# Batch 0's q loaded and prepared by halves of the heads, w2 held behind batch 1's v, and three moves of loads and stores on SP's and GpSimd's queues

## The chip, the cores and the metric

The kernel runs on one core of a Trainium2 chip. The metric is the device time of one execution in microseconds (us); the time before is the median of three runs. Everything said of where time goes comes from one profiled execution. In the listings PE is the matrix engine, PEld its weight loads, DVE the vector engine, ACT the scalar engine, POOL is GpSimd, and SP is the engine that only issues DMA transfers. A "q" behind an engine's name (SPq) is its queue of issued transfers.

## The reference

Eight batches go through a linear attention with cosine weights and then through a mixer with a low-rank part and two dense layers:

```python
# attention, q, k, v of shape (8 batches, 8 heads, 576 rows, 64)
phi(x) = concat([relu(x) * cos_w, relu(x) * sin_w])      # 128 features per head
kv = k_p^T v ;  z = sum over rows of k_p
x = (q_p kv) / (q_p z + 1e-6)                            # 576 x 512 per batch
# mixer
u = x + (low-rank mix over the 576 rows: U, V, rank 32)
out = u + relu(u @ w_ch1) @ w_ch2                        # 512 -> 2048 -> 512
```

The two dense layers are most of the work of PE.

## The kernel before, in words

**Tiling.** The 576 rows of a batch are cut into five chunks: c = 0 to 3 with 128 rows and c = 4, the tail, with 64. Two batches make a pair, whose two tails share one tile. Each of q, k and v has one staging tile in SBUF (qst, kst, vst; 128 x 8 heads x 5 chunks x 64, f32) that all batches use in turn. For batches 0 and 1 it is filled by two loads (`load_odd`, `load_even`, L67 to L77), from batch 2 on by three: `load_tail` for the tail and the two of `load_main` for the other chunks (L79 to L89). All of these are issued by SP. The weights come through POOL's queue (`w1_load`, `w2_load`, L94 to L104), four loads each, with a cast to bf16 in flight.

**The front.** Batch 0 has a path of its own (L813 to L842). 22 dummy matmuls (`keep_warm`) run while q is loaded. `q_prep` then makes the features of a chunk for all eight heads: the cosine half on DVE, the sine half on ACT (on DVE for c = 3). PE transposes each chunk's eight heads (`qtr_mm`), with a dummy matmul behind each chunk; DVE and ACT move the five transposed chunks out of PSUM (`qtr_evac`). `k_prep` follows with the sums z, and `first_chain` does kv, the normalisation, the low-rank part and opens the transposed u (uT) of batch 0.

**What orders the rest.** From there on PE walks a list of slots, written out by hand (L948 to L961), and each engine executes its instructions in the order in which the program gives them. Slots 0 to 15 are the first dense layer of batch 0 (`g1_main`, one slot per 128 of the 2048 columns), 16 to 31 the second layer of batch 0 (`g2_part`, chunks 0 to 3, in four parts that each need one of w2's four loads), 32 to 47 the first layer of batch 1, 48 to 51 that of the two tails, 52 to 71 the second layer for cc = 4 (the tails) and cc = 5 to 8 (batch 1's chunks), four slots each. Slot 72 begins the next pair. Beside the slots hang the steps of the attention of later batches (`put(slot, step)`): the table `PLAN` gives for batches 2 to 7 the slot of kv and the distances of preparing q and k, of the transposes, and of the loads for the batch that follows. Batch 2's kv is at slot 46, batch 3's at 64.

**Transposes by DMA.** From batch 1 on u is transposed by DMA (`utr_dma`, L455), and from batch 2 on q too (`qtr_dma`, L339), all on SP's queue: for batch 3 the q chunks 0 and 1 at slot 59, chunks 2 and 3 at slot 65. The transpose of batch 1's u is at slots 23 and 24, that of batch 2's u at 62 and 64.

**Gates.** POOL issues w1's loads when a small copy (`mark`, L839) has read the last bytes of the first half of batch 0's v, and w2's loads when another (L850) has read the last bytes of batch 1's k. SP holds batch 2's loads at slot 15 with two small transfers that read w2 (`gate`, L867); between these it transposes batch 0's uT back to u (`u_dma`). Batch 2's q (tail and main) and k's tail follow at slot 15; the rest of k, and v, at slot 26.

**Stores.** `g2_part` adds u to the sum in PSUM on DVE (o_sb, four buffers) and stores it: pairs 0 to 2 from POOL's queue, pair 3 from SP's. POOL also casts parts of v to bf16 (`v_prep`); for batch 3 the chunks 4, 0 and 1, at slots 52, 53 and 54.

Of the kernel before, what the change touches and what calls it, by code (L numbers as in the profile page):

```python
# [17 lines left out]
def kernel(  # L18
# [11 lines left out]
    nc = tc.nc  # L30

    B = 8
    H = 8
# [9 lines left out]
    TS = 64  # L43
# [23 lines left out]
    def load_even(dst, src, b, h0=0, h1=H):  # L67
        nc.sync.dma_start(
            out=dst[0:P:2, h0:h1].rearrange("m h c d -> m h (c d)"),
            in_=nines(src, b)[:, h0:h1, 0 : 5 * D],  # L70
        )

    def load_odd(dst, src, b, h0=0, h1=H):
        nc.sync.dma_start(
            out=dst[1:P:2, h0:h1, 0:4].rearrange("m h c d -> m h (c d)"),
            in_=nines(src, b)[:, h0:h1, 5 * D : 9 * D],
        )  # L77
# [38 lines left out]
    stU = st_uv[:, S : S + 5 * R].rearrange("p (c r) -> p c r", r=R)  # L116

    zero = const.tile([P, 512], BF16)
    V_.memset(zero, 0.0)  # L119
    for x in (qst, kst, vst):  # L120
        V_.memset(x[:, :, 4, :], 0.0)
    load_odd(qst, q, 0)
    load_even(qst, q, 0)
    load_odd(kst, k, 0)
    load_even(kst, k, 0)
    for h0 in (0, 4):
# [63 lines left out]
    def keep_warm(n, tag, bufs):  # L190
        w_ps = ps.tile([P, 512], FP32, tag=tag, bufs=bufs, name="w_ps")
        for _ in range(n):
            nc.tensor.matmul(out=w_ps, lhsT=zero[:, 0:P], rhs=zero, start=True, stop=True)  # L193
# [367 lines left out]
        )  # L561

    o_ps = {}

    def g2_part(pr, cc, part):

        last = pr == NPAIR - 1 and cc == 8
        if part == 0 or last and part == 3:
            tag, bufs = ("g", 3) if pr == 0 and 2 <= cc < 4 else ("o", 2)
            o_ps[pr, cc] = ps.tile([P, DM], FP32, tag=tag, bufs=bufs, name="o_ps")  # L570
        o = o_ps[pr, cc]
        if cc == 4:
            b, lhs, c, u = None, hid_tl[pr], 0, u_tl[pr]
        else:
            b, c = (2 * pr, cc) if cc < 4 else (2 * pr + 1, cc - 5)
            lhs, u = hid[b], u_bf[b][:, c, :]

        if last:
            cols = slice(0, 384) if part < 3 else slice(384, DM)
            js = (range(0, 5), range(5, 10), range(10, NJ), range(NJ))[part]  # L580
        else:
            cols, js = slice(0, DM), range(part * 4, part * 4 + 4)
        for j in js:
            nc.tensor.matmul(  # L584
                out=o[:, cols],
                lhsT=lhs[:, j, c * P : c * P + P],
                rhs=w2_bf[:, j, cols],
                start=(j == 0),
                stop=(j == NJ - 1),
            )  # L590
        if js[-1] < NJ - 1:
            return
        o_sb = pool.tile([P, DM], FP32, tag="o_sb", bufs=4, name="o_sb")
        nc.vector.tensor_tensor(  # L594
            out=o_sb[:, cols], in0=u[:, cols], in1=o[:, cols], op=ALU.add
        )
        eng = nc.gpsimd if pr < NPAIR - 1 else nc.scalar if part == 3 and last else nc.sync
        if cc == 4:
            for i in range(2):
                eng.dma_start(  # L600
                    out=out[2 * pr + i].rearrange("(m k) n -> m k n", k=9)[:, 4, :],
                    in_=o_sb[i * TS : i * TS + TS, :],
                )
        else:
            eng.dma_start(  # L605
                out=out[b].rearrange("(m k) n -> m k n", k=9)[:, c : c + 6 : 5, cols],
                in_=o_sb[:, cols],
            )


    def loads(b):
# [29 lines left out]
    def attention_plan(b):  # L641

        plan = []
        w, f_at, q_eng, k_eng, qtr, lo = PLAN[b]

        def put(at, f, *a, tag=False):
            if tag:
                a = a + spare(w + at)
            plan.append((w + at, lambda: f(b, *a)))

        for n, c in enumerate(QORD):
            if b == 3:
                q_eng, k_eng = V_ if n == 3 else A_, A_ if n < 3 else None
                put((-12, -11, -10, -7, -3)[n], q_prep, c, (q_eng, q_eng))
                put(n - 9 if n < 3 else -5, k_prep, c, (A_, k_eng))
                if n > 2:
                    put(2 * n - 12, k_prep, c, (None, V_))
                put(-4 if n > 2 else n - 12, v_prep, 0, H, (c,), (A_ if n > 2 else G_,))
                continue
            put(f_at + n, q_prep, c, (q_eng, q_eng))  # L660
            put(f_at + 6 + n, k_prep, c, (k_eng, k_eng))
            on_v = b == 2 and n > 2
            put(
                -5 if on_v else f_at + 3 + (3 * n) // 2,
                v_prep, 0, H, (c,), (V_ if on_v else G_,),
            )
        for n, (c0, c1) in enumerate(((4, 5), (0, 2), (2, 4))):
            put(1 if b == 3 and n == 2 else qtr + 2 * n, qtr_dma, c0, c1)
        put(0, kv_unit, 0, tag=True)
        put(2, kv_unit, 1, tag=True)  # L670
        for n, c in enumerate(ORD):
            if b > 3:
                put(4 + 2 * n, x_unit, c, "X", 1)
            elif n % 2:
                put(9 if (b, n) == (3, 3) else 4 + (3 * n) // 2, x_two, c, tag=True)
            else:
                put(4 + (3 * n) // 2, x_unit, c, "X", 1)
        a_at = 12 if b < 4 else 14
        put(a_at, A_unit, tag=True)
        odd = b % 2 == 1  # L680
        for c in range(4 + odd):
            put(a_at + 2 + c, u_unit, c, tag=True)
        put(a_at + 4, utr_dma, 0, 2)
        put(a_at + 6, utr_dma, 2, 4)
        if odd:
            put(a_at + 8, utr_dma, 4, 5)
        for at, t in zip(lo, loads(b + 1) if lo else ()):
            plan.append((w + at, t))
        return plan


    TL = (0, 1, 2, 3, 4)
# [119 lines left out]

    FEATS = [(V_, V_ if c == 3 else A_) for c in TL]  # L813
    qT_alloc(0)
    keep_warm(22, "X", 1)
    t_q = []
    for c in TL:
        tg = G3 if c < 3 else O2
        t_q.append(ps.tile([P, H, P], BF16, tag=tg[0], bufs=tg[1], name="t_ps"))
    for c in TL:  # L820
        q_prep(0, c, FEATS[c])
        qtr_mm(0, c, 0, H, t_q[c])
        keep_warm(1, "X", 1)
    for c, eng in zip(TL, (V_, A_, V_, A_, V_)):
        qtr_evac(0, c, eng, t_q[c])
    keep_warm(5, "X", 1)
# [20 lines left out]
    for h0 in (0, 4):  # L847
        load_odd(vst, v, 1, h0, h0 + 4)
        load_even(vst, v, 1, h0, h0 + 4)
    G_.tensor_copy(out=mark, in_=kst[0:TS, 7, 4, 0:1])  # L850
    for n in range(4):
        w2_load(n)
    g1_main(0, 0, True)
# [111 lines left out]
    def put(at, thunk):  # L965
        todo.setdefault(at, []).append(thunk)
# [3 lines left out]
        put(15, lambda c0=c0: u_dma(0, c0, c0 + 2))  # L970
    put(15, lambda: gate(w2_bf[0:1, 4, 0:1]))
    for n, t in enumerate(loads(2)):
        if n == 1:
            put(15, lambda: load_tail(kst, k, 2))
            put(26, lambda: load_main(kst, k, 2))
        else:
            put((15, 0, 26)[n], t)
    for b in range(2, B):
        for at, t in attention_plan(b):
            put(at, t)  # L980
    for i, s in enumerate(slots):
        s()
        for t in todo.get(i, []):
            t()
# [30 lines left out]
```

## Time and profile before

| what | us |
|---|---|
| median of three runs (lowest, highest) | 309.62 (308.99, 310.02) |
| the profiled execution, in all | 310.23 |
| its span, first to last instruction | 308.5 |
| PE busy in the span | 300.3 |
| DVE, ACT, POOL busy | 149.1, 139.5, 52.3 |
| HBM read, written | 36.86 MB, 9.44 MB |

The span is the time that the traces divide; the 1.7 us around it belong to no instruction. Busy time of PE is from the start of a matmul to its modelled end, and matmuls overlap, so the pace of their starts says more than the share. "Landing" is the moment at which all parts of a transfer have signalled. An idle time with an arrow, as in `[2.09 <-DMA vst<-in_v_dram]`, is how long the engine stood before this instruction and what ended the wait. The chain of work lists the pieces that led to the last instruction: start, duration, what. The 40 slices of a row are 7.7 us each.

### The profile page before, as it was taken

To read this page: it belongs to the slowest core of one execution; us is meant where nothing else is said; L and a number is where in the kernel's file an instruction comes from. 1 tells how busy PE (TensorE), PEld (TensorE's weight loads), DVE (VectorE), ACT (ScalarE), POOL (GpSimd) and SP (SyncE) were. 2 spreads that over 40 slices of the span, in tenths; PEclk is the share of its full clock that TensorE was granted. 3 is DMA by queue.
4 is the path that set the end of the run, shared out by engine and by line. 5 is a ranking of instruction groups with operands and counts; after the bars stand their busy time and mean duration, and the time that the engine had idled before them with its cause. 6 is when DMAs were issued, how large, how long until landed. Compare 5 with 4: busy or idle time off the path is not lost.

```text
span 308.5 us, 5730 instructions
## 1 busy us (share of the span) xinstructions
PE 300.3 (97%) x2304; PEld 157.3 (51%) x2329; DVE 149.1 (48%) x354; ACT 139.5 (45%) x237; POOL 52.3 (17%) x94
## 2 busy tenths in 40 slices
PE   8989999999999999999999999999999999999995
PEld 3676464448454444574455444574455444474443
DVE  4978674873866593156336691146327510002111
ACT  2935911365770556579100466679300366630000
POOL 8411200340051007004221400004221000000000
PEclk9999999999999999999999999999999999999999
DMA  7999999999999979991999579912970140001221
GB/s 212 352 261 255 244 193 231 245 328 219 283 216 185 288 142 269 248 260 70 214 208 329 174 124 231 288 39 83 179 166 34 70 85 0 0 2 68 77 95 68
DMA packets 90253, 54.26 MB, mean 176 GB/s; under 512 B 58484, under 2 KB 87444, under 8 KB 90228
## 3 DMA queue, kind: packets, MB, share of 16 engines
q1 hardware_dynamic: 83524, 42.41, 59.7%
q0 software_dynamic: 6560, 11.43, 14.8%
q8 instruction: 18, 0.29, 0.4%
q10 hardware_dynamic: 144, 0.07, 0.1%
q14 instruction: 7, 0.06, 0.1%
HBM read 36.86 MB, written 9.44 MB: 150 GB/s over the span
## 4 chain that ended last, share of the span: by engine, by line
PE 91%; DMA 5%; DVE 2%; issue 1%; ACT 0%; SPq 0%; ACTq 0%; DVEq 0%
PE o_ps L584 38%; PE g_ps L531 36%; PE gt_ps L551 5%; DMA q_pT<-q_p 3%; PE kv_ps L299 3%; PE x_ps L390 2%; DMA qst<-in_q_dram 2%; PE va_ps L435 2%; PE t_ps L328 1%; PE a_ps L415 1%; PE t_ps L316 1%; PE w_ps L193 1%; PE z_ps L832 0%; PE va_ps L438 0%; PE x_ps L894 0%
## 5 line engine op out<-in xcount | busy, mean ns | idle before, releaser
L540 ACT ACTIVATE hid<-g_ps 128x512 bf16<-128x512 f32 x128 | 76.0, 598 | 107.5 <-PE g_ps L531 107.4
L584 PE MATMUL o_ps<-w_bf,hid 128*128 128x512 bf16 (+2 forms) x509 | 117.4, 372 | 0.9
L531 PE MATMUL g_ps<-uT,w_bf 128*128 128x512 bf16 x512 | 116.8, 379 | 0.1
L531 PEld LDWEIGHTS <-w_bf 128*128 128x128 bf16 x512 | 48.6, 98 | 57.2 <-issue 1.7
L584 PEld LDWEIGHTS <-hid 128*128 128x128 bf16 x528 | 48.5, 98 | 51.9 <-issue 1.1
L594 DVE TENSOR_TENSOR o_sb<-u_bf,o_ps 128x512 f32<-128x512 bf16 (+2 forms) x33 | 22.1, 669 | 57.0 <-PE o_ps L584 55.9
L605 POOL DMA_DIRECT2D out_dram<-o_sb x24 | 15.1, 630 | 123.0 <-DVE o_sb L594 60.0
L110 POOL CAST v_ext<-vst 128x512 bf16<-128x512 f32 (+1 forms) x26 | 19.5, 773 | 43.5 <-DMA vst<-in_v_dram 43.3
L110 DVE CAST kv<-kv_ps 128x260 bf16<-128x260 f32 (+1 forms) x15 | 6.4, 429 | 37.4 <-PE kv_ps L299 37.4
L442 DVE TENSOR_TENSOR u_bf<-x_bf,va_ps 128x512 bf16<-128x512 bf16 x24 | 16.5, 686 | 10.2 <-PE va_ps L435 10.2
L363 DVE TENSOR_SCALAR rec<-x_ps 128x8 f32<-128x8 f32 (+2 forms) x39 | 6.3, 162 | 21.2 <-PE x_ps L390 19.4
L551 PE MATMUL gt_ps<-uT_tl,w_bf 128*128 128x128 bf16 x256 | 15.9, 219 | 0.0
L400 DVE TENSOR_TENSOR x_bf<-x_ps,rec 128x512 bf16<-128x512 f32 x22 | 15.2, 692 | 0.8
L551 PEld LDWEIGHTS <-w_bf 128*128 128x128 bf16 x256 | 14.7, 98 | 0.9
L584 PE MATMUL o_ps<-w_bf,hid_tl 128*128 128x512 bf16 x61 | 14.6, 379 | 0.2
L193 PE MATMUL w_ps<-zero 128*128 128x512 bf16 x36 | 11.9, 445 | 1.3 <-DVE zero L119 1.2
L299 PEld LDWEIGHTS <-k_p 128*128 128x128 bf16 x256 | 11.2, 97 | 3.2
L558 ACT ACTIVATE hid_tl<-gt_ps 128x512 bf16<-128x512 f32 x16 | 9.6, 597 | 6.6 <-PE gt_ps L551 6.6
L258 ACT ACTIVATE k_p<-kst,sinw 128x512 bf16<-128x512 f32 x17 | 12.0, 715 | 0.0
L299 PE MATMUL kv_ps<-v_ext,k_p 128*128 128x65 bf16 (+1 forms) x256 | 11.8, 193 | 0.0
L260 DVE TENSOR_SCALAR q_p<-qst,cosw 128x512 bf16<-128x512 f32 x21 | 9.8, 477 | 3.0 <-DMA qst<-in_q_dram 3.0
L390 PEld LDWEIGHTS <-q_pT 128*128 128x128 bf16 x176 | 8.5, 98 | 4.7
(137 smaller groups left out, 245.7 us busy)
## 6 DMA issues: line engine op xcount, KB each, us to landing
qst<-in_q_dram SPq DMA_DIRECT2D x14, 512.0 KB, 5.9
kst<-in_k_dram SPq DMA_DIRECT2D x14, 512.0 KB, 8.0
out_dram<-o_sb POOLq DMA_DIRECT2D x24, 256.0 KB, 4.9
vst<-in_v_dram SPq DMA_DIRECT2D x12, 512.0 KB, 8.8
w_bf<-in_moe_w_ch_dram POOLq DMA_DIRECT2D x8, 512.0 KB, 12.6
out_dram<-o_sb SPq DMA_DIRECT2D x7, 256.0 KB, 2.4
qst<-in_q_dram SPq DMA_DIRECT2D x2, 640.0 KB, 6.5
kst<-in_k_dram SPq DMA_DIRECT2D x2, 640.0 KB
```

The source lines that it names most:

```text
L110: eng.tensor_copy(out=o, in_=i)
L193: nc.tensor.matmul(out=w_ps, lhsT=zero[:, 0:P], rhs=zero, start=True, stop=True)
L299: nc.tensor.matmul(out=acc[:, i, :], lhsT=k_of(b, c, h), rhs=v_tl[:, h, 0:n] if c == 4 and b < 2 else vx[:, c, h, 0:n], start=(c == 0), st ...
L390: nc.tensor.matmul(out=acc[:, g, i * E : i * E + E], lhsT=qT_of(b, c, h), rhs=kv_sb[b][:, h, :], start=True, stop=True,)
L400: nc.vector.tensor_tensor(out=x_of(b, c, rows).rearrange("p (g i d) -> p g i d", g=2, d=D), in0=view[:, :, :, 0:D], in1=rec[rows].unsqueez ...
L442: nc.vector.tensor_tensor(out=u_bf[b][:, c, :] if c < 4 else u_tl[b // 2], in0=x_of(b, c), in1=va, op=ALU.add,)
L531: nc.tensor.matmul(out=g_ps.rearrange("p (c t) -> p c t", c=4), lhsT=w1_bf[:, d, j * P : j * P + P], rhs=uT[b][:, :, d, :], start=(d == 0) ...
L540: nc.scalar.activation(out=hid[b][:, j, :], in_=g_ps, func=AF.Relu, bias=0.0, scale=1.0)
L551: nc.tensor.matmul(out=g_ps[:, jj, :], lhsT=w1_bf[:, d, j * P : j * P + P], rhs=uT_tl[pr][:, d, :], start=(d == 0), stop=(d == 3),)
L584: nc.tensor.matmul(out=o[:, cols], lhsT=lhs[:, j, c * P : c * P + P], rhs=w2_bf[:, j, cols], start=(j == 0), stop=(j == NJ - 1),)
L594: nc.vector.tensor_tensor(out=o_sb[:, cols], in0=u[:, cols], in1=o[:, cols], op=ALU.add)
L605: eng.dma_start(out=out[b].rearrange("(m k) n -> m k n", k=9)[:, c : c + 6 : 5, cols], in_=o_sb[:, cols],)
```

## The change

The change has five parts.

1. Batch 0's q is loaded in four transfers instead of two, heads 0 to 3 first; the zeroing of the staging tile is cut in the same way, the first half ahead of everything. Features and transposes of q are made for heads 0 to 3 of all five chunks, then for heads 4 to 7. There are 10 dummy matmuls ahead instead of 22, and six between instead of five.
2. w2's loads wait for the first half of batch 1's v instead of batch 1's k.
3. Batch 2: of q only the main part is loaded at slot 15; q's tail and all of k go to slot 26 with v, behind the transposes of batch 1's u. The tail of q is prepared last instead of first.
4. Batch 3's casts of v on POOL move from slots 52 to 54 to slot 58.
5. Of pair 0, the stores of cc = 5, 6 and 7 go to SP's queue; those of 5 and 6 are kept back until slot 65, where they follow batch 3's last transpose of q.

```diff
     zero = const.tile([P, 512], BF16)
+    V_.memset(qst[:, 0:4, 4, :], 0.0)
     V_.memset(zero, 0.0)
-    for x in (qst, kst, vst):
+    V_.memset(qst[:, 4:8, 4, :], 0.0)
+    for x in (kst, vst):
         V_.memset(x[:, :, 4, :], 0.0)
-    load_odd(qst, q, 0)
-    load_even(qst, q, 0)
+    for h0 in (0, 4):
+        load_odd(qst, q, 0, h0, h0 + 4)
+        load_even(qst, q, 0, h0, h0 + 4)
...
+    late = []
...
-        else:
+            return
+
+        def store():
             eng.dma_start(
                 out=out[b].rearrange("(m k) n -> m k n", k=9)[:, c : c + 6 : 5, cols],
                 in_=o_sb[:, cols],
             )
+
+        if pr == 0 and 5 <= cc < 8:
+            eng = nc.sync
+            if cc < 7:
+                late.append(store)
+                return
+        store()
...
-                put(-4 if n > 2 else n - 12, v_prep, 0, H, (c,), (A_ if n > 2 else G_,))
+                put(-4 if n > 2 else -6, v_prep, 0, H, (c,), (A_ if n > 2 else G_,))
                 continue
-            put(f_at + n, q_prep, c, (q_eng, q_eng))
+            put(f_at + ((n - 1) % 5 if b == 2 else n), q_prep, c, (q_eng, q_eng))
...
-    keep_warm(22, "X", 1)
+    keep_warm(10, "X", 1)
...
-    for c in TL:
-        q_prep(0, c, FEATS[c])
-        qtr_mm(0, c, 0, H, t_q[c])
-        keep_warm(1, "X", 1)
+    for h0 in (0, 4):
+        for c in TL:
+            q_prep(0, c, FEATS[c], h0, h0 + 4)
+            qtr_mm(0, c, h0, h0 + 4, t_q[c])
+            if c % 2 == 0:
+                keep_warm(1, "X", 1)
...
-    G_.tensor_copy(out=mark, in_=kst[0:TS, 7, 4, 0:1])
+    G_.tensor_copy(out=mark, in_=vst[0:TS, 3, 4, 0:1])
     for n in range(4):
         w2_load(n)
...
     for n, t in enumerate(loads(2)):
-        if n == 1:
-            put(15, lambda: load_tail(kst, k, 2))
-            put(26, lambda: load_main(kst, k, 2))
-        else:
-            put((15, 0, 26)[n], t)
+        if n == 0:
+            put(15, lambda: load_main(qst, q, 2))
+            put(26, lambda: load_tail(qst, q, 2))
+        else:
+            put(26, t)
...
+    put(65, lambda: [store() for store in late])
```

## The prediction

> **What bounds the kernel.** I read the page's first two parts, then PE's waits, then the chain of work in order of time, and last the timelines of POOL and SP where the diff touches them. In the page, PE and its clock are full in every slice but the first and the last:
>
> ```profile
> PE 300.3 (97%) x2304; PEld 157.3 (51%) x2329; DVE 149.1 (48%) x354; ACT 139.5 (45%) x237; POOL 52.3 (17%) x94
> PEclk9999999999999999999999999999999999999999
> ```
>
> From 23 us on PE issues a 512-column matmul each 0.216 us (56 of L531 in 12.19 us from 58.38). A change that takes no matmul away gains only where PE stands still. PE's waits list four places, one of them deep in the kernel; the timeline's chain shows it, and the front in which PE is fed by the loads of batch 0:
>
> ```profile
> PE x_ps L894 <- DMA q_pT<-q_p: 0.7, 1, 0.7
> PE xh_ps L709 <- DVE rec L364: 0.5, 1, 0.5
> ```
>
> ```profile
> 1.70 5.67 DMA qst<-in_q_dram
> 7.48 0.73 ACT q_p L258
> ...
> 12.17 0.89 DVE k_p L260 x2
> 13.09 0.34 PE z_ps L832 x8
> ...
> 23.04 0.43 PE g_ps L531 x2
> ...
> 91.74 9.02 DMA q_pT<-q_p
> 100.81 0.43 PE x_ps L894 x8
> ```
>
> So there are two stretches to win from, the front (0 to 23 us) and the place at 98 to 101 us. All else can only lose.
>
> **1. The place at 98 to 101.** Batch 3's transpose of q chunks 2 and 3 is issued by SP at 91.74 and lands at 100.77, 9.0 us later. The same transpose of batch 4 is issued at 120.77 and lands 4.3 us later, that of batch 2 (68.16) 5.1 us. Just ahead of the slow one stands the transpose of batch 2's u (90.36), 7.8 us to landing, against 4.1 us for batch 1's (52.56). What is different is POOL's list:
>
> ```profile
> 87.71 1.17 POOL L110 CAST v_ext<-vst 128x512 bf16<-128x512 f32 x2 [2.09 <-DMA vst<-in_v_dram]
> 88.83 1.10 POOL L600 DMA_DIRECT2D out_dram<-o_sb  x2
> 89.91 1.28 POOL L605 DMA_DIRECT2D out_dram<-o_sb  x2
> 94.92 0.63 POOL L605 DMA_DIRECT2D out_dram<-o_sb  x1 [3.73 <-DVE o_sb L594]
> ```
>
> The stores of the tails, finished at 81.97, sat behind casts that waited for batch 3's v, and went out with those of cc 5 and 6 onto the transposes. The change puts the casts behind the tails' store (slot 58, that store is slot 55), and cc 5 to 7 on SP behind the transpose (slots 65, 67), in the same ring. I take 5 us for it (bounds 4.3 and 9.0): landed at 96.7. PE wants it at 99.94, eight matmuls after 98.20. PE's start there, 98.20, itself waited for batch 2's uT, landed at 98.15: the step before it ended a matmul slot at 97.96. Gain: 0.24 + (100.81 - 99.94) = **1.11 us**, if PE comes there no later. The two stores held until slot 65 keep two of four o_sb buffers; cc 7 and 8 take the others (cc 8 that of the tails, stored by then), and the next use is at slot 108, so nothing waits. SP gets three issues of 0.65 us ahead of batch 4's loads, but its 6.06 us transpose shrinks by more.
>
> **2. q in halves.** Now the first q_p starts at 7.48, when all q is there (1.70 + 5.67). Packets flow at 350 GB/s and SP's issues (0.65 us each, two more) run 4 us ahead of the data, so the second half lands at 7.4 as before and k where it did (11.15 by its completion signals). The first half lands the second's data time earlier (576 KB at 350 GB/s, 1.7 us): at about 5.7, after cosw (5.02). Per half DVE does six and ACT four instructions. At 128x512 they follow each other every 0.40 and 0.61 us; casts of half width every 0.20 and 0.31 us. So they are through at 7.5 + 6x0.20 = 8.7 instead of 9.92, and after three and two evacuations (0.60, 0.95) at 10.6; before it was 12.17 and 11.82. Then k is late, 11.15: DVE starts it at 11.3, 0.9 us earlier. The path from there to PE's 22.88 is DVE's six k_p, its v casts, and PE and DVE by turns, none of them changed; v's second half (14.46) is wanted at 14.5. So the chain offers 0.9 us (0.5 to 1.1).
>
> The dummy matmuls fall from 22 to 10: first one at 1.45 (zero's memset goes behind one of 0.27 us), 0.43 us each, last end 5.75. In the timeline they are 0.43 us apart until 5.00 and 0.22 from 5.36, so ten are just past the change of rate. If the rate came 3 us later, forty transposes at 0.11 and warm-ups at 0.43 would end near 10.6, still before k: no cost.
>
> **3. What is late next: w1.** The first w1 load (issued 13.03) lands at 13.03 + 8.9 = 21.9, and PE wants it at 22.88. Batch 1's k load, now issued at 14.51, follows batch 0's k_p: it moves to 13.5. Its packets came 3.9 us after the issue (the queue is nearly empty from 17.2 to 18.4), and from then on w1 runs at 117 packets per us instead of 190. One microsecond less alone costs w1 about 0.5: landing 22.4. So only **0.4 us** of the 0.9 reach PE at 23 (bounds 0 and 0.95, the latter if k's packets don't move).
>
> **4. w2 held.** POOL's gate goes from k of batch 1 (28.95) to the first half of v:
>
> ```profile
> 29.07 0.18 POOL L850 COPY mark<-kst 64x1 f32<-64x1 f32 x1 [12.59 <-DMA kst<-in_k_dram]
> 29.52 2.97 POOL L102 DMA_DIRECT2D w_bf<-in_moe_w_ch_dram  x4 [0.27 <-issue]
> ```
>
> That v load, issued at 16.62, lands 16.8 us later, 33.4; with k's loads a microsecond earlier, 32.4. The issue comes 0.57 us later: 33.0. w2's first load took 9.2 us from 29.52 to 38.7, but behind w1 and beside v; a free queue needs some 3.0 us to the first packet (stores: 2.3 to 3.6), 2.6 of data (w2's next loads land 2.5 apart) and up to 1.5 for the last engine: 6.4 to 7.7. So it lands at 39.4 to 40.7; bounds 38.0 and 43.2 (34.0 + 9.2). PE's first o_ps is at 40.57, now 40.2. I take no stall, or 0.4: it eats at most what w1 left. Nothing else stands behind the copy on POOL until 55.6; on SP, the gate on w2 delays u_dma and batch 2's q by about 1.2 us, with 3 us of slack (u_dma lands at 50.44, read at 54.63). Later w2 loads are needed 4 us apart. Batch 1's v gains, but DVE's 2.99 us wait for it cost PE nothing.
>
> **5. Tails behind the transposes.** Two issues of 0.65 us go from before SP's 51.20 to behind 54.63, ahead of batch 2's k and v. DMA is idle at 56.0 to 57.2 (58 GB/s) and absorbs half: v lands 0.5 us later (67.4 to 67.9). q's tail is now prepared last; its transpose waits for SP anyway (63.40). DVE's casts and k_p for kv at 70.41 end at 69.73: 70.2 now. SP is busy without a break to 87.8, so batch 3's v also comes 0.5 us later, and the tails' stores, now under its load, add 0.66. POOL's casts, which end at 88.88, end at 90.0; kv wants them at 89.93. Gain of the front that passes here: **about 0**, with bounds -0.6 and +0.4.
>
> **Sum.** 308.5 - 1.11 - 0 = 307.4 us of span. The profiled execution took 310.23 in all, 1.7 more than its span and 0.6 above the median; on the median this is 309.62 - 1.1 = **308.5**.
>
> **Rivals.**
> (a) The front's gain survives: w1 or v are less late than I make them, and 0.4 to 0.95 is added. For it: DMA lulls; against: three floors in a row. 309.62 - 1.1 - 0.6 = 307.9.
> (b) w2 is late by 1 us: k's packets don't move (34.0) and 7.4 us follow: 41.4 against 40.57. 309.62 - 1.1 + 0.8 = 309.3.
> (c) The transpose stays slow, since its own crowd and not the stores slows it (the one at 221.43, near stores of another pair, took 7.2 us): the stall stays, 309.5.
> (d) Slower: w2 again. Issued at 34.0 with the 9.2 us of now it lands at 43.2, PE stands 2.6 us at its first o_ps: 309.62 - 1.1 + 2.6 = 311.1. It decides from a landing of 40.57 + 1.11 + 0.93 = 42.6.
> (e) Slower: PE stays at the slow rate through the front, because with ten dummies, then transposes with gaps, it isn't busy enough. The chain's PE pieces from 15.7 to 23.9 (kv 0.59, d 0.49, xh 0.41 and 0.48, v 0.32, u 0.38 twice, g 0.43) are 3.5 us and would double: 309.62 - 1.1 + 3.5 = 312.0.
> The Trainium skill, "TensorE: Matmul & The Clock Gate", section "Part 1: The HAM clock gate", holds that full rate is granted after a busy window of about 3.4 us that runs free of the kernel. The trace agrees (1.19 to 5.3 us); by that rule ten dummies suffice only when the window lies well, so (e) has a small chance.
> (f) Halving costs: if each of the two added loads held up the queue for the 2.2 us that a lone 192 KB store takes from issue to landing, k would land at 15.55, DVE start it at 15.6 instead of 12.17: 309.62 - 1.1 + 3.4 = 311.9. Against it: v's halves land 0.75 to 0.92 us apart, their data time.
> The Trainium skill, "DMA: Bandwidth & Descriptors", section "Rules for kernel authors", advises 1 MiB and more per DMA, and its "Anatomy of one DMA — SWDGE (gpsimd) path" puts about 2 us of fixed cost into each; by that figure, an estimate, (f) would be 4 us on k and 311.5. The trace shows such costs overlapped.
>
> **Chances.** Forecast 0.43 (own range 308.1 to 309.0), (a) 0.20, (b) 0.18, (c) 0.07, (d) 0.07, (e) 0.03, (f) 0.02. 0.3% is 0.93 us, about what a measurement can tell from no change; below 308.69 is faster: three quarters of the forecast, (a), a little of (b): 0.55. Slower: (d), (e), (f): 0.12. The rest, 0.33, is the same. Range 307.5 to 309.9, which leaves out the ends of (a) and (d) to (f).
>
> **What would show it.** Right: the transpose at 91 lands within 6 us, PE's waits lose L894, POOL's tail stores go out near 82; q_p begins near 5.7, DVE's k_p near 11.3, PE's first L531 at 22.4 to 22.6, its first o_ps at 40.2 to 40.6, kv of batch 3 near 90. Wrong: a wait of PE for w_bf at 40, for v_ext at 70 or 90, or matmuls 0.43 us apart behind 9 us.

## The result, and the profile after

The changed kernel takes **311.97 us** (median of 11 runs, 310.17 to 313.77), the kernel before 309.62: a ratio of 1.0067, 95% interval 1.0045 to 1.0089. Forecast were 308.5 us and a range of 307.5 to 309.9. The profiled execution took 312.16 us with a span of 310.4, 1.9 more than that of before.

From the page of the changed kernel, PE's row and the row of the instruction queue (packets, MB, share), which becomes important below; and from PE's waits, three of the rows that are new (us in total, times, longest):

```profile
PE 299.3 (96%) x2293; PEld 156.4 (50%) x2318; DVE 151.8 (49%) x361; ACT 140.6 (45%) x241; POOL 50.6 (16%) x91
q8 instruction: 18, 0.29, 0.4%
```

```profile
PE g_ps L534 <- DMA w_bf<-in_moe_w_ch_dram: 1.9, 1, 1.9
...
PE v_ps L229 <- issue: 0.7, 1, 0.7
...
PE kv_ps L302 <- POOL v_ext L110: 0.2, 1, 0.2
```

The wait for q_pT, 0.7 us before, is gone; in its place PE stands nearly 2 us at its first matmul on w1. The chain of work, in order of time, says what w1 waited for, and further on where v of batches 2 and 3 holds PE:

```profile
13.71 1.53 POOL mark L854
15.25 10.15 DMA w_bf<-in_moe_w_ch_dram
25.45 0.60 PE g_ps L534 x2
```

```profile
61.80 9.20 DMA vst<-in_v_dram
...
73.34 0.67 PE kv_ps L302 x17
...
92.54 0.62 POOL v_ext L110
...
93.20 0.73 PE kv_ps L302 x19
```

Setting the same matmul of both timelines side by side gives the whole account. The last column says what the step belongs to.

| PE's matmul | before, us | after, us | lead or lag | step |
|---|---|---|---|---|
| xh_ps, ahead of the idle time of before | 18.40 | 18.49 | +0.09 | the front: no gain |
| xh_ps, second group | 19.36 | 19.04 | -0.32 | before stands 0.46 us here, after does not |
| xh_ps, after v_ps | 20.05 | 20.60 | +0.55 | idle at v_ps, 0.87 |
| first g_ps | 22.88 | 25.45 | +2.57 | waits for w1, 2.02 |
| g_ps after the first kv of batch 2 | 71.02 | 73.85 | +2.83 | v of batch 2, 0.26 |
| o_ps after the first kv of batch 3 | 90.75 | 93.99 | +3.24 | v of batch 3, 0.41 |
| x_ps of the stall | 100.81 | 102.92 | +2.11 | the stall of before is not there, -1.13 |
| last groups (285 us on) | | | +2.10 | nothing more |

So PE came to the place at 98 to 101 3.24 us late, 2.57 of them from before 26 us, and 1.13 us of the lag went there, as many as forecast. That is a comparison with one execution of before, the one with the stall; whether the change won them is taken up under stores_only. The row at 18.40 says that halving q gave PE nothing: the lead at 19.36 is idle time of before, which the changed kernel has a little later, at v_ps.

### The profile page after: what moved, and what is told of

It is laid out like the page before. It is cut to its first block, busy times and chain, and to the rows that moved or that the text cites. A ratio compares the mean times of both kernels' runs of the same rounds, so it can differ in the third digit from the quotient of the medians.

```text
span 310.4 us, 5721 instructions
## 1 busy us (share of the span) xinstructions
PE 299.3 (96%) x2293; PEld 156.4 (50%) x2318; DVE 151.8 (49%) x361; ACT 140.6 (45%) x241; POOL 50.6 (16%) x91
## 4 chain that ended last, share of the span: by engine, by line
PE 83%; DMA 10%; SPq 2%; DVE 2%; issue 1%; POOL 1%; DVEq 0%
PE o_ps L588 37%; PE g_ps L534 32%; DMA vst<-in_v_dram 6%; PE gt_ps L554 5%; DMA w_bf<-in_moe_w_ch_dram 3%; PE kv_ps L302 3%; PE x_ps L393 2%; PE va_ps L438 2%; DMA qst<-in_q_dram 1%; PE a_ps L418 1%; SPq L74 1%; PE t_ps L319 1%; SPq L87 1%; DVE u_bf L952 1%; POOL mark L854 0%
## 5 line engine op out<-in xcount | busy, mean ns | idle before, releaser
L534 PE MATMUL g_ps<-uT,w_bf 128*128 128x512 bf16 x512 | 116.8, 379 | 1.9 <-DMA w_bf<-in_moe_w_ch_dram 1.9
L534 PEld LDWEIGHTS <-w_bf 128*128 128x128 bf16 x512 | 48.6, 98 | 58.9 <-DMA w_bf<-in_moe_w_ch_dram 2.0
L611 POOL DMA_DIRECT2D out_dram<-o_sb x21 | 13.2, 630 | 127.5 <-DVE o_sb L598 59.1
L110 POOL CAST v_ext<-vst 128x512 bf16<-128x512 f32 (+1 forms) x26 | 18.4, 729 | 31.7 <-DMA vst<-in_v_dram 28.5
L366 DVE TENSOR_SCALAR rec<-x_ps 128x8 f32<-128x8 f32 (+2 forms) x39 | 6.3, 162 | 20.1 <-PE x_ps L393 19.4
L302 PEld LDWEIGHTS <-k_p 128*128 128x128 bf16 x256 | 11.3, 97 | 3.5 <-issue 0.3
L263 DVE TENSOR_SCALAR q_p<-qst,cosw 128x512 bf16<-128x512 f32 (+1 forms) x25 | 12.1, 504 | 1.4 <-DMA qst<-in_q_dram 1.4
L196 PE MATMUL w_ps<-zero 128*128 128x512 bf16 x25 | 9.9, 482 | 1.6 <-DVE zero L120 1.5
L261 ACT ACTIVATE q_p<-qst,sinw 128x512 bf16<-128x512 f32 (+1 forms) x17 | 10.4, 633 | 2.2 <-DMA qst<-in_q_dram 2.2
```

The lines of the kernel that those rows point to most:

```text
L110: eng.tensor_copy(out=o, in_=i)
L261: nc.scalar.activation(out=o, in_=i, func=AF.Relu, bias=0.0, scale=w)
L263: eng.tensor_scalar(out=o, in0=i, scalar1=0.0, scalar2=w, op0=ALU.max, op1=ALU.mult)
L302: nc.tensor.matmul(out=acc[:, i, :], lhsT=k_of(b, c, h), rhs=v_tl[:, h, 0:n] if c == 4 and b < 2 else vx[:, c, h, 0:n], start=(c == 0), st ...
L534: nc.tensor.matmul(out=g_ps.rearrange("p (c t) -> p c t", c=4), lhsT=w1_bf[:, d, j * P : j * P + P], rhs=uT[b][:, :, d, :], start=(d == 0) ...
L611: eng.dma_start(out=out[b].rearrange("(m k) n -> m k n", k=9)[:, c : c + 6 : 5, cols], in_=o_sb[:, cols],)
```

## Experiments

All were timed in five rounds against the kernel before, on the same chip.

### One part at a time

**no_halves**: all of the change but q in halves (the memsets, loads, 22 dummies and q_prep as before).

> Everything of the change but the halves: q of batch 0 in two loads, 22 dummy matmuls, features by whole chunks. Theory H (the halves lose the time, through loads that land later and through w1's gate on GpSimd): the front is that of before, the first matmul of L531 at 22.9 us, no wait for w1; the stall at 98 to 101 us is gone (-1.1), of which the later v of batches 2 and 3 may take back up to 0.6: 308.5 to 309.1, ratio 0.9965 to 0.9985. Theory D (fewer dummy matmuls, so that the full rate is granted later) gives the same here. Theory W (w2's later gate, the moved tails and stores lose it): still 311 to 312.

Measured: 311.58 us (before 309.58), ratio 1.0067 (1.0044 to 1.0090). So the halves are not the only cause: the rest alone costs as much. The front is as before (first g_ps at 22.77). w2 is issued at 34.24, behind batch 1's v (33.67), and lands at 39.96, before its first o_ps at 40.46: PE does not wait for w2. PE's waits show what is late instead:

```profile
PE g_ps L531 <- DMA uT<-u_bf: 0.6, 1, 0.6
PE kv_ps L299 <- POOL v_ext L110: 0.5, 2, 0.4
PE kv_ps L299 <- DVE v_ext L110: 0.4, 1, 0.4
```

**halves_only**: q in halves with ten dummies, the rest as before.

> The kernel before with the halves alone (four loads of q, the zeroing cut, features and transposes by halves, 10 dummy matmuls). Theory H: second half of q lands near 8.9 instead of 7.4, w1's first load near 25.4, a wait of PE of some 2 us before the first matmul of L531; 312.0 or so, ratio 1.006 to 1.010. Theory D: the same time, but with a rate granted late. Theory W: no slower than before, 309.6.

Measured: 311.35 us (before 309.58), ratio 1.0060 (1.0028 to 1.0091). w1 is issued at 15.00 and lands at 26.0; PE's wait, and a row of the windows view (the stretch, its length, busy time per engine, granted clock, DMA share, GB/s) with the clock taken back just after it:

```profile
PE g_ps L534 <- DMA w_bf<-in_moe_w_ch_dram: 3.0, 1, 3.0
```

```profile
27.00:30.50 3.50, 3.50 (x13) 1.40 (x12) 2.57 (x6) 1.88 (x4) 0.19 (x1) 0.51 1.18 246
```

The two halves of the change do not add: each costs 1.8 to 2.0 us alone, both together 2.35. In the changed kernel w1 gets into the queue late, so batch 1's v lands at 28.50 instead of 33.43, and w2, held for v, is issued at 29.07 as before. The late w1 pays for w2.

**stores_only**: batch 3's v casts at slot 58 and the late stores on SP, nothing else.

> The kernel before with the last two parts alone: batch 3's casts on GpSimd at slot 58, and three stores of batch 1 on SP behind batch 3's transpose. The prediction's first step: batch 3's transpose of chunks 2 and 3 lands within 6 us of its issue, PE's wait at 100.8 is gone, batch 3's kv is not held: 308.5, ratio 0.9964. Rival (the transposes slow themselves): the wait stays, 309.6. Second rival (the tails' stores, now under batch 3's v loads, hold kv): 308.5 to 309.3 with a wait of PE for v_ext near 90.

Measured: 309.08 us (before 309.58), ratio 0.9991 (0.9974 to 1.0008); in its profile the span is 307.2 and x_ps of the stall 1.20 us earlier. The median is 0.5 us lower, the ratio 0.3, and the interval reaches from 0.8 us faster to 0.25 slower: a gain on the median is not shown. Nor does the stall stand in every execution: **before_w1k** and **before_pad** below have the code of before there, with the same stores on POOL; PE comes 0.80 and 0.39 us later than in before, does not wait for q_pT, and is ahead of before behind the place. The matmul of the stall in before, then in before_w1k:

```profile
100.81 0.43 PE L894 MATMUL x_ps<-kv,q_pT 128*128 128x65 bf16 x8 [0.71 <-DMA q_pT<-q_p]
```

```profile
100.48 0.42 PE L894 MATMUL x_ps<-kv,q_pT 128*128 128x65 bf16 x8
```

The mechanism holds all the same: from issue to landing this transpose takes 5.1 to 9.0 us in the eleven profiles without this part of the change (median 7.4) and 4.3 to 5.7 in the seven with it (median 4.9). The 9.02 us of before are the slowest of all.

**w2_only**: the gate on w2 alone.

```
-    G_.tensor_copy(out=mark, in_=kst[0:TS, 7, 4, 0:1])
+    G_.tensor_copy(out=mark, in_=vst[0:TS, 3, 4, 0:1])
     for n in range(4):
         w2_load(n)
```

> The kernel before with the second part alone: w2's loads wait for the first half of batch 1's v. Everything but the halves cost 2 us, with waits of PE for batch 1's transposed u at 57 us and for v at 71 and 92 us. Theory G (w2's gate does it: SP's gate on w2, and batch 2's loads behind it, move by 1.2 to 4 us): these waits are here, 310.5 to 311.5. Theory T (the moved tails do it): 309.6, no waits.

Measured: 313.47 us (before 309.76), ratio 1.0113 (1.0069 to 1.0158), the costliest part alone. w2 lands at 39.84, PE does not wait for it, but SP does: the issues of the gate, of u_dma (4.57 us for its second half instead of 3.96) and of batch 2's loads end at 51.31, and the transposes of batch 1's u stand behind them. The first one's issue takes 2.75 us instead of 1.26, the second moves from 52.56 to 54.22. In the chain of work:

```profile
50.89 3.32 PE o_ps L584 x16
54.22 4.99 DMA uT<-u_bf
...
59.34 1.83 PE g_ps L531 x4
```

Before, this transpose landed at 56.62 and PE's first matmul on it started at 57.02: a slack of 0.40, not 3. PE stood 2.4 us, and then the granted clock was 0.50 from 59.41 to 62.82.

**tails_only**: batch 2's q and k tails behind the transposes, and q's tail prepared last.

> The kernel before with the third part alone: batch 2's q tail, k tail and the rest of k behind batch 1's transposes, its q tail prepared last. Theory T: two more transfers ahead of batch 2's k and v on SP's queue, v 0.5 to 1.3 us later, waits of PE for v at 71 and 92 us; 310.3 to 311.3. Theory G: 309.6, at most 0.3 us of wait for v.

Measured: 310.56 us (before 309.76), ratio 1.0027 (0.9998 to 1.0056). The transposes land earlier (55.88), v of batch 2 later: 69.25 instead of 67.38. PE loses 0.93 us at 71 to 72, though the interval of the time reaches down to no loss. This fits no_halves, which costs 2.0 us and not the 3.7 of w2_only: in its trace the wait for uT is 0.6 us instead of 2.4, and the waits for v are 0.9; the tails give the transposes back a part of what w2 takes, and pay with v.

### Why w1 is late in the halves

In the changed kernel POOL's copy, which releases w1, took 1.59 us; it took 0.22 before. The timelines of POOL, then of DVE:

```profile
13.71 1.59 POOL L854 COPY mark<-vst 64x1 f32<-64x1 f32 x1 [5.14 <-DMA vst<-in_v_dram]
```

```profile
14.70 0.56 DVE L110 CAST v_ext<-vst 128x768 bf16<-128x768 f32 x1
15.58 0.17 DVE L110 CAST z_sb<-z_ps 128x8 bf16<-128x8 f32 x1 [0.32 <-PE z_ps L847]
```

The copy ends at 15.30, when DVE's unbroken row of six k_p and a v cast ends (15.26). The same in halves_only (15.06 and 15.02) and halves_fill (14.96 and 14.92). The Trainium skill, "SBUF — State Buffer", section "Who interferes with whom", has GpSimd share a pair of ports with DVE, which copies, casts and `tensor_scalar` can take, in certain modes, for a whole instruction while the other blocks. The trace agrees, with one thing more: the block lasted over three to four DVE instructions that overlap each other. In the kernel before the copy began 0.09 us ahead of the next k_p and got through at once; there it was a k_p that took longer, 0.70 instead of 0.48 us, beside POOL's issue of w1. What decides between the two isn't settled. How far ahead of the next k_p the copy begins does not: it was 0.20 us in the changed kernel, where the copy was held, and in tails_only, where it got through in 0.33 us.

**halves_dmagate**: halves_only, but the gate on w1 is a small GpSimd transfer of the same element, not a copy.

> The halves alone, with w1's gate on GpSimd changed from a copy of 64 values of v to a transfer of the same values, which GpSimd issues and does not compute. Theory P (the copy is held up on GpSimd while DVE works without a break: it took 1.6 us where it took 0.2 before): w1's first load is issued some 0.7 us behind v's landing, at 13.5 to 14.4 instead of 15.0 to 15.3, lands near 23.5 instead of 25.4 to 26.0, and the time falls by 1 to 2 us against the halves alone: 309.6 to 310.4. Rival (v's later landing alone does it, 12.8 to 13.7): w1 stays at 25 or later, 311 to 311.5.

Measured: 313.66 us (before 309.76), ratio 1.0130 (1.0088 to 1.0172). POOL's rows: the transfer's issue is held up as the copy was (1.23 us), so the theory that the form of the gate is to blame fell.

```profile
13.56 1.23 POOL L844 DMA_DIRECT2D mark<-vst  x1 [5.03 <-DMA vst<-in_v_dram]
14.77 1.89 POOL L96 DMA_DIRECT2D w_bf<-in_moe_w_ch_dram  x2
```

w1, issued at 14.77, lands at 25.66, 10.9 us later; batch 1's k is in the queue ahead of it (issued 13.87, landed 20.37; before 14.51 and 23.90). PE waits 3.3 us. That the time is 2.3 us above halves_only, with w1 no later, fits the clock: all six runs have a mean granted clock of 0.995 or below, against 7 of 12 there.

**halves_w1k**: halves_only, with w1 released by batch 0's k.

```
-    G_.tensor_copy(out=mark, in_=vst[0:TS, 3, 4, 0:1])
+    G_.tensor_copy(out=mark, in_=kst[0:TS, 7, 4, 0:1])
     for n in range(4):
         w1_load(n)
```

> Only the first part of the change (q in halves, 10 dummies), and w1's four loads are released by batch 0's k instead of the first half of its v. In the halves alone k landed at about 11.7 and v's first half at 13.34, GpSimd's copy began at 13.39 and lasted 1.67 us, w1 was issued at 15.00 and landed at 26.0, PE waited 3.16 us. Theory L (w1's issue is what makes the halves slow: it comes after batch 1's k is in the queue): the copy begins at 11.8 to 12.1, w1 is issued at 12.1 to 12.6 before batch 1's k (14.0), lands 8.9 us later as it did in the kernel before, 21.0 to 21.8, and PE does not wait for w_bf; first L534 at 22.2 to 23.0; 309.0 to 309.9 us. Rival B (the halves cost by themselves, through the later landings of q's second half, k and v): PE's wait for w_bf is gone, but the first L534 is at 23.5 or later and the time stays above 310.5. Rival P (GpSimd's copy is held up wherever it stands beside DVE's casts): the copy lasts 1.4 us or more again, w1 is issued at 13.5 to 13.8 and lands at 22.4 to 23.5; PE waits up to 0.5 us, 309.8 to 310.4.

Measured: 310.35 us (before 309.72), ratio 1.0014 (0.9997 to 1.0030). Theory L holds for two thirds of the cost, 1.1 of 1.8 us: the copy falls ahead of DVE's k_p, beside a copy out of PSUM (q_tlT, 11.58 to 12.26), takes 0.18 us, and PE no longer waits for w1 (landed 22.75). Its bounds on landing and time were missed: the first g_ps stands at 23.55, where rival B had it, and another wait is in PE's list:

```profile
11.94 0.18 POOL L844 COPY mark<-kst 64x1 f32<-64x1 f32 x1 [3.42 <-DMA kst<-in_k_dram]
12.06 3.73 POOL L96 DMA_DIRECT2D w_bf<-in_moe_w_ch_dram  x4
```

```profile
PE v_ps L229 <- issue: 0.9, 1, 0.9
```

**before_w1k**: the kernel before with the same line changed.

> The kernel before with the same earlier release of w1 and nothing else: it tells whether the earlier release has a price or a gain of its own. k landed at 11.15, so w1 is issued at 11.5 instead of 13.03 and lands at 20 to 21 instead of 21.91. PE's first L531 at 22.88 did not wait for w1 there, so by theory L nothing is won: 309.3 to 309.9. Rival B: w1's packets reach the queue beside v's second half (14.46, wanted at 14.5) and make it late by 0.3 to 1 us: first L531 at 23.2 to 23.9, 309.9 to 310.6.

Measured: 309.98 us (before 309.72), ratio 1.0011 (0.9992 to 1.0030): no gain, at most a small price. The first g_ps, at 23.67, and the time lie where rival B had them, but 0.5 of the 0.8 us come at the idle time taken up below (0.74 us here, 0.46 in before).

### Dummies and the clock

**halves_22**: halves_only with all 22 dummies.

> The halves alone, but with the 22 dummy matmuls of before ahead of them. Theory D: the full rate is granted near 5.3 us again and the loss goes: 309.0 to 309.6. Theory H: the loads and w1's gate are as late as with ten, since neither hangs on PE: 311.5 to 312.2, perhaps with less scatter from run to run.

Measured: 311.10 us (before 309.58), ratio 1.0051 (1.0026 to 1.0075). The copy took 0.18 us, w1 was issued at 12.96 and landed at 21.77, but in the profiled run the granted clock was 0.50 from 20.43 to 27.26 and DVE began k at 12.95. The first g_ps stands at 27.10. So w1's lateness can go and the time stay; but the profile shows one execution, the slowest of the twelve, and the runs spread from 309.49 to 313.39.

**halves_fill**: halves_only with eight dummies ahead of the first g_ps, so that PE is busy while it waits for w1.

> The halves alone, with eight dummy matmuls (1.7 us) ahead of the first matmul that needs w1. Theory C (while PE waits for w1, its clock is taken back for a window of 3.4 us, which costs up to 1.7 us more in about half of the runs): no run with a lowered clock behind 20 us, the slowest runs (313.7 to 314.3) are gone, median 311 to 311.5. Rival (the lowered clock comes from the sparse front, not from the wait): lowered clocks as before, and 1.7 us more where w1 is not late: 312 to 313.

Measured: 311.82 us (before 309.76), ratio 1.0059 (1.0032 to 1.0086): no gain on the median. The mean granted clock was 0.995 or below in 2 of 12 runs, against 7 of 12 without the filling. That speaks for the clock being taken back where PE waits for w1; it is no proof, with so few runs, and it is not the only way: halves_22 above and halves_w1k_pad below lose the clock without a wait for w1.

### Putting parts together

**after_w1k**: the whole change, with w1 released by batch 0's k.

> The whole changed kernel with one line different: w1's loads released by batch 0's k. With that the halves alone cost next to nothing (310.35 against 309.72). Theory S (the parts' prices don't add, since w1's lateness hid w2's): w1 is in the queue before batch 1's loads again and lands at 21.5 to 22.8, PE does not wait for it; but batch 1's v lands at 33.5 to 34.5 instead of 28.50, w2 is issued at 34 to 35, its first load lands at 40 to 41 and the following SP instructions are late as in the kernel without the halves: waits of PE for uT near 57 (0.3 to 0.8 us) and for v of batches 2 and 3 near 71 and 91 (0.2 to 0.6 each); 310.8 to 311.9 us, as without the halves (311.58). Rival A (the prices add): the changed kernel's 311.97 less the 1.0 to 1.3 us that the earlier release took off the halves alone gives 310.7 or less, with no wait for uT.

Measured: 310.74 us (before 310.00), ratio 1.0035 (1.0009 to 1.0061). Theory S has the mechanism: v of batch 1 lands at 33.47 again, w2 is issued at 34.05, and the waits that the late w1 had hidden come back. The front is that of before: w1 lands at 21.79 (21.91 in before) and the first g_ps stands at 22.88, as there.

```profile
PE kv_ps L302 <- DVE v_ext L110: 0.4, 1, 0.4
PE g_ps L534 <- DMA uT<-u_bf: 0.3, 1, 0.3
```

The time, 0.06 us below its bound and 0.04 above the rival's, doesn't tell the two apart. The one line halves the ratio's excess over 1; the two intervals overlap, and the first g_ps, 2.57 us earlier than in the changed kernel, is the firmer sign.

**halves_w1k_stores**: the halves, w1 released by k, batch 3's v casts and the late stores.

> q in halves with w1 released by batch 0's k, and the parts on batch 3's v casts and the late stores; batch 2's loads and w2's gate as in the kernel before. Theory S: nothing is late in front beyond what the halves with the earlier release showed, and the place at 98 to 101 loses its stall (0.44 us there): 309.4 to 310.0 us, no better than the stores alone (309.08), since k, not q, sets the front. Rival F (a gain of the front passes once nothing behind takes it): first L534 at 22.5 or before and 308.7 or less.

Measured: 309.70 us (before 310.00), ratio 0.9994 (0.9976 to 1.0011). As theory S has it: no better than the stores alone.

### The idle time of 0.4 to 0.9 us at 19 to 21 us

One row of PE's timeline before, one after:

```profile
19.36 0.28 PE L709 MATMUL xh_ps<-kv,q_tlT 128*128 128x64 bf16 x4 [0.46 <-DVE rec L364]
```

```profile
20.47 0.20 PE L229 MATMUL v_ps<-V_nat,four 32*128 32x64 bf16 x1 [0.70 <-issue]
```

DVE's rec had been done since 17.3, so the name in brackets is not the cause. Counting PE's matmuls and weight loads, and the ten to fourteen of its instructions that only wait, 447 to 449 of them stand ahead of the end of the idle time in 13 of the 14 traces so far (not in w2_only), whatever line stands there, and it ends 1.23 to 1.48 us after the end of a packet of 16 KB of the instruction queue: before, the packet ran from 16.85 to 17.98, after, from 17.93 to 19.08. The queue's 18 packets would hold PE's 4,600 matmuls and weight loads at 256 each, and from one packet to the next PE moves on by some 245 instructions. Theory I: PE waits for its own code. Then 80 more short instructions early must move the wait to another line, and the count stay.

```
+    def keep_short(n):
+        w_ps = ps.tile([P, 512], FP32, tag="X", bufs=1, name="w_ps")
+        for _ in range(n):
+            nc.tensor.matmul(
+                out=w_ps[:, 0:8], lhsT=zero[:, 0:P], rhs=zero[:, 0:8], start=True, stop=True
+            )
...
-    keep_warm(22, "X", 1)
+    keep_warm(17, "X", 1)
+    keep_short(45)
```

**before_pad**: the kernel before with this edit.

> The kernel before with 80 more short PE instructions early: of the 22 dummy matmuls five give way to 45 of 8 columns (45 matmuls and 45 weight loads), about the same time. In the profiles so far PE stands still at its 447th to 449th instruction in all kernels (matmuls and weight loads counted), 1.23 to 1.48 us after a 16 KB packet of the instruction queue has ended, whatever line stands there: in the kernel before at 19.36, the fetch from 16.85 to 17.98, some 2.9 us after PE passed its 191st instruction (13.95). Theory I (PE waits for its own code): with 80 instructions more, the 191st is reached near 10.8 instead of 13.95 and the packet begins at 13.4 to 14.6; PE comes to its 448th instruction at 17.7 to 17.9 (the second kv of batch 0), the packet having ended by 16; the 0.46 us of idle time before L709 is gone, first L531 at 22.3 to 22.6 instead of 22.88, 308.9 to 309.5 us. Rival D (PE waits there for DVE's rec, as the list of waits says): the idle time of 0.4 to 0.5 us stays at the same line L709, first L531 at 22.8 or later, no gain.

Measured: 310.02 us (before 310.11), ratio 0.9998 (0.9973 to 1.0022). The packet runs from 13.45 to 14.59, PE passes its 448th instruction at 18.23 without a pause, and the idle time before L709 is gone. By this the wait was for code. The time missed its forecast: in this execution DVE began k 0.79 us later (why is open), and what the code gave (0.4) went there. The first g_ps stands at 23.26.

**halves_w1k_pad**: halves_w1k with keep_short(40) between the transposes of q's halves.

> q in halves with w1 released by batch 0's k, and 80 short PE instructions (40 matmuls of 8 columns) between the two halves' transposes. Without them PE stood still 0.86 us before L229 (19.74 to 20.60), 1.48 us after the instruction packet (18.16 to 19.12); up to there it was 0.35 us ahead of the kernel before, behind it 0.68 late. Theory I: the packet begins at 13 to 15, the idle time before L229 is gone, the first L534 at 22.5 to 22.8 instead of 23.55, limited next by w1 (landed 22.75); 309.3 to 310.0 us, 0.4 to 0.9 below the halves with the earlier release alone. Rival B (the halves' later data, v's second half at 15.2, is what holds the chain there): idle time at L229 stays at 0.6 or more; first L534 at 23.4 or later, 310.3 or more.

Measured: 310.70 us (before 310.11), ratio 1.0021 (1.0003 to 1.0038). The packet came no earlier than 17.10, and the idle time moved with the count: it is now before instruction 449 at another line, 1.27 us after the packet's end (18.08).

```profile
PE kv_ps L309 <- issue: 1.0, 1, 1.0
```

That rules out v's second half as the cause of the idle time at L229. The first L534, at 25.15, and the time lie where rival B had them all the same: PE lost 1.0 us here, and from 21.70 on the granted clock was 0.50, with no wait for w1 ahead of it:

```profile
21.70:25.10 3.40, 3.40 (x38) 2.02 (x35) 1.67 (x4) 1.75 (x5) 0.00 (x0) 0.50 1.17 254
```

Why the packet starts 5.8 us after PE passed its 191st instruction here, and 2.2 us in before_pad, is not settled; w1's packets, released at 12.27 here and at 13.82 there, are the likely ones in its way. One pair of runs points there: before_w1k moves w1's release alone, from 13.03 to 11.82, and its packet starts 3.6 us after that instruction, 2.9 in before.

**stores_pad** and **halves_w1k_stores_pad**: the edit of before_pad on stores_only, that of halves_w1k_pad on halves_w1k_stores.

> The late stores and batch 3's v casts alone (309.08 without the short instructions, idle time 0.30 us at PE's 447th instruction), with the same 80 short PE instructions as in the kernel before. Theory I: the idle time is gone, 0.2 to 0.4 us less than without, 308.7 to 308.9. Rival D: 309.1 as without them.

> q in halves, w1 released by batch 0's k, the late stores and batch 3's v casts, and the 80 short PE instructions: all that the runs so far leave of the change without a price. Theory I: no idle time at L229, first L534 at 22.4 to 22.9, 308.4 to 309.2 us, below the kernel before (309.6 to 310.0) and near or below the late stores alone. Rival B: 309.7 as without the short instructions.

Measured: 309.71 us (before 310.11), ratio 0.9983 (0.9967 to 0.9999), and 310.85, ratio 1.0035 (1.0016 to 1.0055). Both miss theory I's bounds, though the idle time is gone in the first; in the second it stands at the same count as in halves_w1k_pad (1.0 us). No version of this study is faster than the kernel before by more than 0.2%; the stores alone, with or without the short instructions, come nearest.

## Why the prediction was wrong, point by point

The sum was one gain of 1.11 us, with nothing lost anywhere else. In the changed kernel's profile the rest lost 3.24 us, 2.0 of them at w1.

- **"The place at 98 to 101"**, the only gain in the sum: right in the mechanism, wrong in the size. The transpose landed in 5.49 us (5 forecast), and SP's issue of it shrinks from 6.06 us:

```profile
95.15 2.21 SPq L345 DMA_TRANSPOSE q_pT<-q_p  x1
97.81 2.16 SPq L611 DMA_DIRECT2D out_dram<-o_sb  x3
```

  That the account has -1.13 for the 1.11 forecast is luck. The gain was read from the one execution in which the transpose was slowest: the other ten profiles without this part of the change lose 0.7 to 1.1 us of lag there too, seven of them 1.0 to 1.1, and on the median stores_only shows no gain that is clear of the spread (0.5 us, ratio 0.9991). And a landing at a fixed time is no cost to a PE that comes later: in the changed kernel, 3.24 us late, the old transpose would hardly have been waited for.
- **"q in halves": failed.** The first half came early (5.20, forecast 5.7). The second half landed at 8.86, not 7.4, k at 12.0, not 11.15, and DVE began k at 12.33, not 11.3. DVE came to it without a break from its last evacuation, so that it was q's second half that set the 12.33, not k, which the prediction had as late:

```profile
11.73 0.68 DVE L110 COPY q_tlT<-t_ps 128x512 bf16<-128x512 bf16 x1
12.33 1.67 DVE L263 TENSOR_SCALAR k_p<-kst,cosw 128x512 bf16<-128x512 f32 x4
```

  The windows view, before and then after, shows one reason for the late landing, less data from 4 to 7 us (last figure, GB/s):

```profile
4.00:7.00 3.00, 3.00 (x12) 1.24 (x11) 0.46 (x3) 1.01 (x3) 2.82 (x11) 1.00 1.08 346
```

```profile
4.00:7.00 3.00, 2.74 (x13) 1.12 (x12) 2.14 (x6) 2.71 (x7) 2.82 (x11) 1.00 0.99 306
```

  The other is the last of 16 completions: those of q's second half are 1.9 us apart, those of the whole q were 0.4. "The second half lands when all of q did" took the sum of bytes for the landing. In the ten kernels with the halves DVE's first k_p stands between 11.7 and 13.0, against 12.17 before.
- **The rest of the chain, "none of them changed": failed.** Of the "0.9 us" PE had, at 18.5 us, between 0.54 and nothing in six of the halves' profiles (in the changed kernel 0.09 too little). What came next was the wait for code. The profile of before has it too (0.46, given to rec), so that all six seem 0.3 to 0.95 us ahead at 19.4; but their own follows at v_ps, at a later line of the program, since there are fewer dummies ahead. It moves PE back by 0.35 to 1.03 us, 0.87 in the changed kernel, against 0.41 in before. The prediction had no such term.
- **"What is late next: w1": failed, and this is the largest term.** The prediction let it cost half of the front's gain; it cost 2.0 us, as much as the whole difference of the two profiled executions. The prediction kept w1's issue at 13.03 and moved batch 1's k to 13.5 ("landing 22.4"). The gate waits for v's first half, which came 0.85 us later (13.66); the copy was then held up 1.4 us more beside DVE; and from its issue, at 15.25, it took 10.15 us instead of 8.9, with batch 1's k, issued at 14.46, already in the queue (how much of that is k's no run separates). after_w1k undoes this alone: the first g_ps is back at 22.88, and the time falls by 1.2 us, by 1.1 in the halves alone (halves_w1k).
- **"w2 held"**: the landing was right where the front is as before (39.84 and 39.96, forecast 39.4 to 40.7; no stall). The slack behind it was wrong: "3 us", read from u_dma, while the transposes behind it on SP had 0.40. In the changed kernel none of it shows, because v landed at 28.50.
- **"Tails behind the transposes"**: right in kind, small in size. v of batch 2 is later by 1.9 us alone, not 0.5, and kv waits 0.93; in the changed kernel 0.26, and 0.41 at batch 3.
- **The rivals.** (d), slower by w2, named the wrong load. (e), the slow clock in the front, did not come as told, since the rate was granted by 6.8 us; what came is a clock taken back behind a wait, in some executions: 5 of the 11 runs of the changed kernel have a mean of 0.995 or below and are 1.25 us longer on average. The Trainium skill, "TensorE: Matmul & The Clock Gate", section "Part 1: The HAM clock gate", has the rate fall back after an idle window of about 3.4 us; the trace shows a stretch of 3.41 us at half rate (halves_only, 27.06 to 30.48), but after a wait of 3.0, and others after shorter ones (below). (f), the cost of halving, had the result (311.9) by luck: k landed at 12.0, not 15.55. The figure cited beside it is one for GpSimd's transfers; q's are SP's.

## What to carry to other kernels

Before a load is moved forward, follow every gate that hangs on the loads behind it, up to the engine that opens it and what this engine shares with its neighbours; a gate that waits for the next tensor in the queue inherits each delay ahead. Read the slack of a queue at its last instruction, not at the one that is moved. Where the profile names a releaser that was done long ago, or "issue", compare the idle time with the packets of the instruction queue before a gain is counted across it.

## What the runs showed of the hardware

- PE waits for its own code. In a stretch where it runs many short instructions while the DMA queues are full, the wait is 0.2 to 1.3 us; the packet of 16 KB began 2.2 to 5.8 us after PE had passed the instruction 256 places ahead of the one that it waits for. The Trainium skill, "Runtime: NRT & Kernel Launch", section "Instruction fetch mechanics", gives blocks of 16 KiB and 256 instructions, as the 18 packets here, and calls the cost mostly hidden; here it is not, and the measurement decides. That it is code that PE waits for is inferred from the count and from the runs that moved it.
- GpSimd's copy of 64 elements took 0.18 to 0.54 us, or 1.41 to 1.67 us in the three runs where DVE's unbroken row of k_p held it to its end; the issue of a GpSimd transfer was held up in the same way (1.23 us). What decides is open.
- After a wait of PE of 2.4 to 3.3 us the granted clock was 0.50 for one stretch of 3.41 us (halves_only, w2_only, halves_dmagate). Shorter ones had it too: 3.41 us, from 2.4 us after a wait of 1.0 (halves_w1k_pad), and 6.83 us, from the middle of one of 1.3 (halves_22). In the changed kernel's own profile, with 1.9 us, the clock stayed.
- Batch 3's second DMA transpose of q, with GpSimd's stores just ahead of it and beside it, took a median of 7.4 us from issue to landing (eleven profiles, 5.1 to 9.0), 4.9 without them (seven, 4.3 to 5.7).
